# Start-up of a transformer block on one core: row tiles of x in transfers of their own, two modulation columns ahead of a transpose, one load fewer for V

## The chip, the core and the metric

The kernel runs on one core of a Trainium2 chip. The time is the device time of one execution in microseconds (us). All times inside an execution are counted from the start of its profiled span. The kernel before takes 1272.2 to 1272.4 us (medians of the jobs), and its executions on one chip lie mostly within 0.3 us of each other. The question here is about some tenths of a microsecond in the first 15 us, so the profile, which shows single events, weighs more than the timed runs. The granted clock of the tensor engine (PE) was 0.997 to 1.000.

## The reference

The reference is one block with conditioning (adaLN), attention over a cached window, and a gated feed-forward part. Only its beginning matters here.

```python
mod = (silu(c) @ w_mod)          # six vectors of 1024: sa, ca, ga, sb, cb, gb
h = layernorm(x) * (1 + ca) + sa # x: 2048 x 1024, bf16
q = h @ wq                       # 1024 x 4096: 32 heads of 128
k, v = the last 512 rows of the caches, 4 kv groups
x = x + ga * (softmax(q k^T / sqrt(128)) v @ wo)
h = layernorm(x) * (1 + cb) + sb
x = x + gb * (silu(h @ w_gate) * (h @ w_up) @ w_down)
```

## The kernel before: the parts that matter

The kernel works through x in four chunks of 512 rows, each of four row tiles of 128 rows. Tiles 0 to 3 of the first chunk stand at the very start: nothing useful can run on PE until they are loaded, normalised and transposed. SyncE issues all these loads in program order on one queue.

```python
def load_x2(i):                     # two row tiles, 512 KB, one transfer
    fetch(out=x2t[i], in_=x2d[2*i*P:2*(i+1)*P, :].rearrange("(t p) d -> p t d", p=P))

for i in range(QT // 2):            # tiles 0+1, then tiles 2+3
    load_x2(i)
for half in range(DH):
    load_wm(1, half)                # w_mod columns of ca: 1 MB, rows of 1 KB
    load_wq8(2 * half)              # weights of q, 512 KB each, rows of 2 KB
    load_wq8(2 * half + 1)
load_wm(0, 0)                       # w_mod columns of sa
...
load_wm(0, 1)
# [cut: V of group 0, two loads of wq, the transposed K]
for kv in range(1, Hkv):            # V of kv groups 1 to 3, two loads each
    load_v(kv, 0, WT // 2)
    load_v(kv, WT // 2, WT)
```

The work on the four tiles is dealt out to three engines. VectorE (DVE) takes the statistics of tiles 0, 2 and 3. ScalarE (ACT) takes sum and squares of tile 1, and 1/std of all four. GpSimd (POOL) normalises tiles 0 and 1, VectorE tiles 2 and 3. `warm(n)` are matmuls whose result is thrown away.

```python
stats_0(0); act_sum(1)              # DVE: tile 0.  ACT: sum of tile 1
nc.scalar.copy(out=siluc, in_=sil_ps)
rstd_0(0)                           # ACT, needs DVE's statistics of tile 0
stats_0(2); act_squares(1)
warm(3)
xpose_0(0, norm_0(0))               # POOL normalises, PE transposes (h_ps)
rstd_0(1, 1.0 / D); rstd_0(2)
warm(5)
stats_0(3)
xpose_0(1, norm_0(1))
xpose_0(2, ln_norm(2))              # DVE normalises
rstd_0(3)
n3 = ln_norm(3)
mod_cols(1, 0, ca1, True, (0,))     # PE: column 0 of 1+ca (mod_ps), then DVE: modT
xpose_0(3, n3)
# [cut: the tiles hs and the helper h_scale]
h_scale(0, h0_ps[0][:, 0, :])       # DVE: hs = h * (1+ca), what the first q needs
nc.scalar.copy(out=h10[:, 4:8, :], in_=h0_ps[1])
mod_cols(1, 0, ca1, True, (1,))
h_scale(1, h0_ps[0][:, 1, :])
mod_cols(1, 0, ca1, True, (2, 3))
h_scale(2, ...); h_scale(3, ...)
for dt in (0, 2):                   # DVE: copies of hT, which free a buffer for matmul results (PSUM)
    nc.vector.tensor_copy(out=h10[:, dt:dt+2, :], in_=h0_ps[0][:, dt:dt+2, :])
# then q of heads 4 to 6 (12 matmuls), then of head 0 in the buffer freed above
```

A `chain` over this whole first phase keeps program order on every engine.

## Time and profile before

| | before |
|---|---|
| time, median of the first 3 runs | 1272.22 us (1272.18 to 1272.53) |
| profiled span | 1270.4 us |
| tiles 0 and 1 of x landed | 4.48 us |
| tiles 2 and 3 of x landed | 5.83 us |
| PE transposes of tile 1 begin | 9.94 us |
| first q matmul | 12.10 us |

A landing here is the moment of the last of the 16 increments of a transfer's semaphore (the counter that the engines wait on), as the trace records them; the first increment came at 3.79 us for tiles 0 and 1 and at 5.12 us for tiles 2 and 3.

The page of the kernel before, busy time of each engine:

```profile
PE 1262.5 (99%) x7589; PEld 641.2 (50%) x7589; DVE 609.4 (48%) x1332; ACT 335.0 (26%) x440; POOL 4.2 (0%) x15
```

PE is busy for 99% of the span, so the start can only be worth the time by which PE's stream begins earlier. What sets that moment is read in the chain of waits that ended last, first 13 us, kernel before (columns: start, duration, what):

```profile
0.73 3.74 DMA x<-in_A_x_dram
4.50 1.30 DVE st L846 x2
...
6.07 0.30 ACT mv L966
...
6.72 1.25 ACT junk L982 x2
...
8.69 1.20 POOL xn L990
...
9.94 1.07 PE h_ps L961 x16
11.01 0.18 PE mod_ps L786 x8
11.19 0.47 PE h_ps L961 x8
11.66 0.58 PE mod_ps L786 x24
12.23 0.89 PE q_ps L1043 x4
```

Tile 0's statistics (`st`) wait for the joint transfer; ScalarE's chain over tile 1 (`mv`, `junk`) follows; GpSimd's rows of tile 1 (`xn`) come next; then PE has work without a pause: transposes (`h_ps`), modulation columns (`mod_ps`) and q (`q_ps`). (PE's starts in this view are modelled ends of the piece before, so the first q matmul shows as 12.23 here; its own start is 12.10.) The timeline of the kernel before shows what stood beside that chain (the bracket gives the idle time before an instruction and what ended it):

```profile
5.56 0.14 ACT L996 COPY siluc<-sil_ps 128x8 bf16<-128x8 bf16 x1
...
5.95 1.23 DVE L846 BATCH_NORM_STATS2 st<-x 128x6 f32<-128x512 bf16 x2
6.07 0.29 ACT L966 ACTIVATE mv<-mv,eps_t 128x1 f32<-128x1 f32 x1 [0.36 <-DVE mv L848]
...
8.97 1.64 DVE L865 TENSOR_SCALAR xn<-x,mv 128x1024 bf16<-128x1024 bf16 x2 [0.16 <-ACT mv L967]
...
12.10 3.73 PE L1043 MATMUL q_ps<-hs,wq 128*128 128x512 bf16 x16
...
14.79 0.33 PEld L1043 LDWEIGHTS <-wq 128*128 128x128 bf16 x3 [0.43 <-DVE hT L1032]
```

ScalarE waited for the statistics of tile 0: its copy of siluc ended at about 5.70, 1/std of tile 0 began at 6.07. VectorE began with tile 2 at 5.95 us, 0.12 us after tiles 2 and 3 had landed (5.83). And PE's thirteenth q matmul had to wait for the copies of hT: 12 matmuls of 0.216 us from 12.10 would end at 14.69, it began at 14.79.

### The profile page before, as it was taken

Reading aid. Unit: us, or ns where it says so; the run is one execution under the profiler, and the core shown is the slowest. Engines: PE = TensorE matmul, PEld = TensorE weight load, DVE = VectorE, ACT = ScalarE, POOL = GpSimd, SP = SyncE. Lnnn points to the kernel's source line nnn. Section 1 sums busy time; section 2 is a strip of 40 time slices with the busy share of each in tenths; the row PEclk is TensorE's granted clock in tenths of the full one; section 3 lists DMA queues with packets and bytes.
Section 4 is the critical chain, followed back from the end, with each engine's and each line's share of the span. In section 5 each row is a group of like instructions: output and inputs, shape, how many; then the busy total and the mean of one; then the engine's idle time right before and its main releaser. Section 6 shows DMA issues by size and latency. Waiting matters only on the chain.

```text
span 1270.4 us, 18154 instructions
## 1 busy us (share of the span) xinstructions
PE 1262.5 (99%) x7589; PEld 641.2 (50%) x7589; DVE 609.4 (48%) x1332; ACT 335.0 (26%) x440; POOL 4.2 (0%) x15
## 2 busy tenths in 40 slices
PE   8999999999999999999999999999999999999998
PEld 4555555555555555555554444444444444444444
DVE  5666658785678664677564631321122112221122
ACT  3543334343333433334341111011100111011100
POOL 1000000000000000000000000000000000000000
PEclk9999999999999999999999999999999999999999
DMA  9897667768456655454575478336633565425702
GB/s 293 204 246 188 163 141 175 166 161 222 120 137 175 150 137 154 113 154 113 121 203 146 132 229 248 95 95 209 213 115 106 169 211 183 158 91 168 246 14 72
DMA packets 306763, 204.45 MB, mean 161 GB/s; under 512 B 145521, under 2 KB 303217, under 8 KB 306674
## 3 DMA queue, kind: packets, MB, share of 16 engines
q1 hardware_dynamic: 301762, 199.03, 57.7%
q10 hardware_dynamic: 4912, 4.20, 1.0%
q8 instruction: 61, 1.00, 0.3%
q14 instruction: 28, 0.23, 0.1%
HBM read 165.94 MB, written 4.21 MB: 134 GB/s over the span
## 4 chain that ended last, share of the span: by engine, by line
PE 99%; DMA 0%; ACT 0%; DVE 0%; POOL 0%; issue 0%; POOLq 0%
PE gu_ps L1358 30%; PE a_ps L1276 17%; PE q_ps L1201 16%; PE d_ps L1378 15%; PE o_ps L1244 9%; PE s_ps L1212 9%; PE q_ps L1043 1%; DMA x<-in_A_x_dram 0%; PE one_ps L1061 0%; PE mod_ps L786 0%; PE h_ps L961 0%; PE one_ps L1054 0%; DVE st L846 0%; ACT junk L982 0%; POOL xn L990 0%; ACT mv L966 0%
## 5 line engine op out<-in xcount | busy, mean ns | idle before, releaser
L1214 ACT ACTIVATE pT<-s_ps 128x1024 bf16<-128x1024 f32 x256 | 249.3, 1020 | 347.5 <-PE s_ps L1212 347.5
L1276 PE MATMUL a_ps<-wo,oT 128*128 128x512 bf16 x1024 | 241.9, 379 | 0.0
L1201 PE MATMUL q_ps<-hT,wq 128*128 128x512 bf16 x960 | 227.1, 379 | 0.0
L1364 DVE TENSOR_TENSOR guT<-gu_ps,sg 128x512 bf16<-128x512 f32 x112 | 77.4, 691 | 286.9 <-ACT sg L1363 286.9
L1358 PE MATMUL gu_ps<-hT,wg 128*128 128x512 bf16 x896 | 211.7, 379 | 0.0
L1363 ACT ACTIVATE sg<-gu_ps 128x512 bf16<-128x512 f32 x112 | 66.9, 597 | 488.7 <-PE gu_ps L1358 483.0
L1378 PE MATMUL d_ps<-wd,guT 128*128 128x512 bf16 (+2 forms) x952 | 194.2, 366 | 0.0
L1358 PE MATMUL gu_ps<-hT,wu 128*128 128x512 bf16 x672 | 163.3, 379 | 0.0
L1276 PEld LDWEIGHTS <-oT 128*128 128x128 bf16 x1024 | 100.2, 98 | 120.6
L947 DVE CAST qT<-q_ps 128x512 bf16<-128x512 f32 x121 | 83.6, 691 | 154.9 <-PE q_ps L1201 154.7
L1201 PEld LDWEIGHTS <-wq 128*128 128x128 bf16 x960 | 93.9, 98 | 113.3
L1378 PEld LDWEIGHTS <-guT 128*128 128x128 bf16 x952 | 90.9, 98 | 103.0
L1244 PEld LDWEIGHTS <-pT 128*128 128x128 bf16 x2048 | 126.6, 98 | 30.2
L1358 PEld LDWEIGHTS <-wg 128*128 128x128 bf16 x896 | 87.6, 98 | 105.5
L1244 PE MATMUL o_ps<-v_sb,pT 128*128 128x129 bf16 x2048 | 137.0, 220 | 0.0
L1212 PE MATMUL s_ps<-qT,kT 128*128 128x512 bf16 x512 | 131.6, 379 | 0.0
L1358 PEld LDWEIGHTS <-wu 128*128 128x128 bf16 x672 | 65.8, 98 | 79.3
L1231 DVE TENSOR_TENSOR oq<-o_ps,rl 128x256 bf16<-128x256 f32 (+2 forms) x256 | 100.6, 419 | 3.9
L1382 DVE TENSOR_TENSOR f<-d_ps,gb_bc 128x512 f32<-128x512 f32 (+2 forms) x34 | 22.4, 660 | 139.8 <-PE d_ps L1378 139.8
L1212 PEld LDWEIGHTS <-kT 128*128 128x128 bf16 x512 | 44.9, 98 | 30.9 <-issue 0.5
L1284 DVE TENSOR_TENSOR acc<-a_ps,acc 128x512 f32<-128x512 f32 x64 | 44.0, 687 | 32.6 <-PE a_ps L1276 32.6
L1358 PE MATMUL gu_ps<-hT,v_sb 128*128 128x512 bf16 x224 | 57.5, 379 | 0.0
(101 smaller groups left out, 427.3 us busy)
## 6 DMA issues: line engine op xcount, KB each, us to landing
wq<-in_A_wq_dram SPq DMA_DIRECT2D x64, 512.0 KB
wo<-in_A_wo_dram SPq DMA_DIRECT2D x64, 512.0 KB
wg<-in_B_w_gate_dram SPq DMA_DIRECT2D x56, 512.0 KB
wd<-in_B_w_down_dram SPq DMA_DIRECT2D x56, 512.0 KB
wu<-in_B_w_up_dram SPq DMA_DIRECT2D x42, 512.0 KB
v_sb<-in_B_w_up_dram SPq DMA_DIRECT2D x14, 512.0 KB
x<-in_A_x_dram SPq DMA_DIRECT2D x8, 512.0 KB
wm<-in_w_mod_dram SPq DMA_DIRECT2D x4, 1024.0 KB
```

The lines of the kernel that those rows point to most:

```text
L947: nc.vector.tensor_copy(out=t, in_=q_ps)
L1201: nc.tensor.matmul(q_ps, lhsT=w, rhs=hT[("h1", cc)][:, dt, :], start=(dt == 0), stop=(dt == DT - 1))
L1212: nc.tensor.matmul(s_ps[:, i, :], lhsT=kT[:, kv, j * P:(j + 1) * P], rhs=qT[g], start=True, stop=True)
L1214: nc.scalar.activation(out=p[:, 2 * jj:2 * jj + 2, :], in_=s_ps, func=ACT.Exp, scale=scale)
L1231: nc.vector.tensor_tensor(out=dst, in0=ps[:, s0:s0 + cnt, 0:Dh], in1=sc, op=ALU.mult)
L1244: nc.tensor.matmul(o_slot["ps"][:, s_, :], lhsT=pT[g][:, j, t * P:(t + 1) * P], rhs=v_sb[:, kv, j, 0:VN], start=(j == 0), stop=(j == WT - 1))
L1276: nc.tensor.matmul(a_ps, lhsT=oT[(cc, 2 * q + i)][:, hh % 4, t * P:(t + 1) * P], rhs=wo_tiles[(cc, q, dh, i)][:, hh % 4, :], start=(hh == ...
L1284: nc.vector.tensor_tensor(out=acc[(cc, t)][:, dsl], in0=a_ps, in1=acc[(cc, t)][:, dsl], op=ALU.add)
L1358: nc.tensor.matmul(ps[:, n, :], lhsT=gu_w[(cc, fg, nm, dt // 4)][:, dt % 4, fi * P:(fi + 1) * P], rhs=hT[("h2", cc)][:, dt, :], start=(dt ...
L1363: nc.scalar.activation(out=g, in_=ps[:, 0, :], func=ACT.Silu)
L1364: nc.vector.tensor_tensor(out=guT[(cc, fg)][:, fi, :], in0=ps[:, 1, :], in1=g, op=ALU.mult)
L1378: nc.tensor.matmul(d_ps, lhsT=guT[(cc, f // 4)][:, f % 4, t * P:(t + 1) * P], rhs=wd_tiles[(cc, dh, f // 4)][:, f % 4, c0:c0 + w], start=( ...
```

## The change

The intent: tile 0 is there earlier when it does not share a transfer with tile 1, so that ScalarE's wait goes; two columns of 1+ca are ready before the last transposes, so that VectorE can scale without alternating with PE; and V of kv group 1 takes one load in place of two. The whole diff:

```diff
-    for i in range(QT // 2):
-        load_x2(i)
+    for tt in range(2):
+        fetch(out=xt[tt], in_=x2d[tt * P:(tt + 1) * P, :])
+    load_x2(1)
@@
-    for kv in range(1, Hkv):
+    load_v(1)
+    for kv in range(2, Hkv):
         load_v(kv, 0, WT // 2)
         load_v(kv, WT // 2, WT)
@@
     mod_cols(1, 0, ca1, True, (0,))
+    mod_cols(1, 0, ca1, True, (1,))
     xpose_0(3, n3)
@@
-    mod_cols(1, 0, ca1, True, (1,))
     h_scale(1, h0_ps[0][:, 1, :])
```

The order of instructions on every engine is otherwise the same, through the whole kernel.

## The prediction

> **What bounds the kernel.** One core, span 1270.4 us, and the tensor engine (PE) is busy 99% of it (busy summary). PE's waits (list of waits) are 3.2 us: 1.6 us before the first matmul and 1.6 us for normalised rows in the first 10 us; behind VectorE's copies of hT it loses 0.11 more (14.684 to 14.790). From 9.94 us on PE runs nearly without gap, so the change is worth what it brings PE's stream forward: tenths of a microsecond.
>
> **The chain before** (chain of waits, first 12 us): x tiles 0 and 1 land in one 512 KB transfer at 4.48; VectorE statistics of tile 0, 4.50 to 6.04; ScalarE rstd 0, 6.07 to 6.59, mean and squares of tile 1 to 7.97, rstd 1 to 8.53; GpSimd normalises tile 1, 8.69 to 9.89; PE transposes from 9.94. ScalarE had waited 0.36 us (5.71 to 6.07) for statistics of tile 0: only that can be gained.
>
> **Row tiles in own transfers.** The landing records show the two x transfers 1.35 us apart (4.48, 5.83), so half a transfer is 0.67 us: tile 0 should land at about 3.8, tile 1 still at about 4.5, tiles 2 and 3 at about 5.85. The Trainium skill, "DMA: Bandwidth & Descriptors" (why a DMA increments its semaphore by 16), says that only the full count tells of landing, so the joint transfer did hold tile 0 back. Statistics of tile 0 then end at 5.4, but ScalarE is bound by tile 1 (sum until 5.7): its chain gains 0.35 us, not 0.67. GpSimd's rows of tile 1 end at about 9.54. VectorE's statistics of tiles 2 and 3 gain under 0.1: tile 2 landed at 5.83 for a start at 5.95. Normalising tile 2 on VectorE took 1.19 us against 0.53 for tile 3 because it overlapped GpSimd (the Trainium skill, "SBUF — State Buffer", calls the shared ports an exclusive lock); it ended 0.28 after GpSimd, so it moves along.
>
> **Modulation columns earlier.** Same matmuls (0.2 us), moved ahead of the transposes of tile 3. With tile 1 ready 0.35 earlier, the transposes of tile 3 come only 0.15 earlier, and the first scaled rows (hs, 0.48 us after them) bind the first q matmul: about 11.88 instead of 12.10, with a new PE stall of about 0.14 us. But VectorE no longer alternates hs and modT, so its copies of hT end about 14.39 instead of 14.73, and the 0.11 us stall at 14.79 goes. Total: q of head 0 starts about 14.47 instead of 14.79, **0.3 us earlier**. Thereafter PE bound; the weights have slack (second half of w_mod's shift columns lands at 24.5, needed at 25.7).
>
> **V of kv group 1 in one load.** One issue fewer at 28 to 32 us, first used some 30 us later: 0.
>
> The main phase keeps its order on every engine, so the gain stays.
>
> **Predicted: 1271.9 us, 80% range 1271.2 to 1272.6.** Faster by over 2%: 0.005; within 2%: 0.99; slower by over 2%: 0.005.
>
> **Right if** the profile after shows VectorE's first statistics at about 3.85, ScalarE's rstd 0 at about 5.72, PE's transposes of tile 1 at 9.6, first q matmul at about 11.9, no stall behind the hT copies, all later work 0.3 us earlier. **Wrong if** the split transfers land no earlier (fixed latency rules), tile 1 or tiles 2 and 3 land later by over 0.2 us, a weight tile lands too late for PE; the spread of three runs (0.35 us) can hide it.

## The result and the profile after

The changed kernel took 1272.71 us (median of 6 runs, 1272.34 to 1274.64), the kernel before 1272.41 us in the 6 runs beside it. The ratio of the two is 1.0003 with a 95% interval of 0.9991 to 1.0016. (A ratio is the mean time of one kernel's fast runs over that of the other's of the same rounds, so not quite the ratio of the medians.) The median lies 0.1 us above the range that I had given, and the small difference has the other sign: I expected 0.3 us less. By the interval of one job this could be noise. It repeated: two further jobs gave medians of 1272.73 against 1272.38 and 1272.76 against 1272.25.

| | before | after | forecast for after |
|---|---|---|---|
| tile 0 landed | 4.48 (with tile 1) | 3.50 | 3.8 |
| tile 1 landed | 4.48 | 4.15 | 4.5 |
| tiles 2 and 3 landed (first part, last part) | 5.12, 5.83 | 5.39, **7.68** | 5.85 |
| ScalarE's 1/std of tile 0 | 6.07 | 5.27 | 5.72 |
| PE transposes of tile 1 | 9.94 | 9.14 | 9.6 |
| VectorE's statistics of tile 2 | 5.95 | **7.70** | about 5.9 |
| first q matmul | 12.10 | 12.91 | 11.88 |
| q of head 0 (thirteenth matmul) | 14.79 | 15.50 | 14.47 |
| profiled span | 1270.4 | 1271.1 | |

The chain of waits that ended last, first 13 us, kernel after:

```profile
0.74 0.40 SPq L664
...
1.19 0.42 SPq L664
...
1.66 6.01 DMA x<-in_A_x_dram
7.70 1.30 DVE st L848 x2
...
9.23 1.16 DVE st L848 x2
...
10.54 0.51 DVE xn L867
...
11.09 0.62 PE h_ps L963 x8
11.71 0.38 PE mod_ps L788 x16
12.09 0.47 PE h_ps L963 x8
12.56 0.38 PE mod_ps L788 x16
12.94 0.35 PE q_ps L1045
```

ScalarE and GpSimd are gone from it. The chain now starts with the third transfer, 6.01 us from its issue to its last part, and goes on with VectorE's statistics of tiles 2 and 3 (`st` twice) and its rows of tile 2 (`xn`). The timeline of the kernel after shows that the part that I had aimed at did work:

```profile
3.53 1.28 DVE L848 BATCH_NORM_STATS2 st<-x 128x6 f32<-128x512 bf16 x2 [1.98 <-DMA x<-in_A_x_dram]
...
5.23 0.14 ACT L998 COPY siluc<-sil_ps 128x8 bf16<-128x8 bf16 x1
5.27 0.29 ACT L968 ACTIVATE mv<-mv,eps_t 128x1 f32<-128x1 f32 x1
...
7.70 1.29 DVE L848 BATCH_NORM_STATS2 st<-x 128x6 f32<-128x512 bf16 x2 [2.64 <-DMA x<-in_A_x_dram]
...
9.14 0.62 PE L963 MATMUL h_ps<-ident,xn 128*128 128x128 bf16 x8 [0.23 <-POOL xn L992]
...
11.09 0.62 PE L963 MATMUL h_ps<-ident,xn 128*128 128x128 bf16 x8 [1.33 <-DVE xn L867]
...
12.91 2.97 PE L1045 MATMUL q_ps<-hs,wq 128*128 128x512 bf16 x12
```

ScalarE's wait is gone (no bracket at 5.27), and PE has tile 1 0.80 us earlier. The starts follow the landings by 0.02 to 0.03 us (3.50 and 3.53, 7.68 and 7.70), so the full count of 16 is indeed what the engines wait for. But VectorE then waits 2.64 us for tile 2, and PE waits 1.33 us for the rows of tile 2 (11.09). Before, tiles 2 and 3 landed 0.12 us ahead of need, so nearly all of their delay reached VectorE, and enough of it reached PE (the sum is below) that what the other chain had won went unused.

From there on both traces run in parallel. I compared every weight load of PE in the two traces: from the second half of the first phase (26 us) to the last one of the block the offset stays between +0.69 and +0.70 us. So nothing later gives or takes anything, and V of kv group 1, whose load falls at 28 to 34 us, cost or gained nothing that can be seen. The end of the kernel, behind the start of the last matmul, varies from profile to profile (4.83 to 5.19 us), and with it the span.

How fast the transfers ran is read from the windows view. The columns that matter are the last two: the busy share of the transfer engines and GB/s. The first part of the line is the window. First the kernel before, then the kernel after:

```profile
1.50:3.50 2.00, 1.91 (x5) 0.69 (x5) 0.04 (x2) 1.44 (x4) 0.26 (x1) 1.00 0.80 229
3.50:6.50 3.00, 3.00 (x10) 0.82 (x8) 1.96 (x4) 1.60 (x5) 0.52 (x5) 1.00 1.02 370
6.50:9.50 3.00, 1.61 (x14) 0.85 (x13) 2.77 (x7) 2.72 (x10) 2.16 (x3) 1.00 1.08 357
```

```profile
1.50:3.50 2.00, 1.91 (x5) 0.69 (x5) 0.05 (x2) 1.45 (x4) 0.24 (x1) 1.00 0.68 252
3.50:6.50 3.00, 2.63 (x10) 0.72 (x8) 1.49 (x3) 2.27 (x7) 1.08 (x6) 1.00 0.81 227
6.50:9.50 3.00, 2.06 (x20) 1.22 (x21) 1.76 (x4) 1.40 (x5) 2.02 (x3) 1.00 1.06 373
```

Between 3.5 and 6.5 us the transfer engines moved 370 GB/s before and 227 GB/s after, and they were partly idle although loads were waiting behind. I call this the slow stretch. It does not hit the 16 parts of a transfer alike: the first part of tiles 2 and 3 landed at 5.39, the last at 7.68. The packet records of this stretch show two things: most packets kept their usual 84 ns for 2 KB, with gaps of some 0.5 us and more between them, and some took 300 to 700 ns. (The records name neither transfer nor engine. That the gaps lie between the packets of tile 1 and those of tiles 2 and 3 is concluded from their times, 3.4 to 4.0 us.)

### The profile page after: what moved, and what is told of

Its sections match the earlier page's. It is cut to its first block, busy times and chain, and to the rows that moved or that the text cites. A ratio compares the mean times of both kernels' runs of the same rounds, so it can differ in the third digit from the quotient of the medians.

```text
span 1271.1 us, 18012 instructions
## 1 busy us (share of the span) xinstructions
PE 1254.6 (99%) x7447; PEld 641.2 (50%) x7589; DVE 609.0 (48%) x1332; ACT 335.2 (26%) x440; POOL 4.2 (0%) x15
## 4 chain that ended last, share of the span: by engine, by line
PE 98%; issue 1%; DMA 0%; DVE 0%; SPq 0%
PE gu_ps L1360 30%; PE a_ps L1278 17%; PE q_ps L1203 16%; PE d_ps L1380 15%; PE o_ps L1246 9%; PE s_ps L1214 9%; PE q_ps L1045 1%; DMA x<-in_A_x_dram 0%; DVE st L848 0%; PE one_ps L1063 0%; PE mod_ps L788 0%; PE one_ps L1056 0%; PE h_ps L963 0%; SPq L664 0%; DVE xn L867 0%
```

## Experiments

Theories at the start: (A) the late landing is chance and differs between executions; (B) the split itself causes it. Later: (S) whatever comes third, behind two short transfers, is starved; (P) it is the paired shape behind single tiles; (O) it is the third transfer of the queue, whatever precedes; (K) it is the cut to short transfers of 256 KB; (W) it is w_mod's many short rows queued behind. All kernels gave correct results. The five jobs ran on five chips; each table compares runs of one job, so of one chip.

### 1. Repeats and the parts of the change alone

`before_again` and `after_again` are the two kernels unchanged. `x_only` and `mod_only` are the kernel before with one part of the change:

```diff
 x_only:
-    for i in range(QT // 2):
-        load_x2(i)
+    for tt in range(2):
+        fetch(out=xt[tt], in_=x2d[tt * P:(tt + 1) * P, :])
+    load_x2(1)
 mod_only:
     mod_cols(1, 0, ca1, True, (0,))
+    mod_cols(1, 0, ca1, True, (1,))
     xpose_0(3, n3)
     ...
-    mod_cols(1, 0, ca1, True, (1,))
     h_scale(1, h0_ps[0][:, 1, :])
```

> The kernel before, unchanged, for a second profile. Theory A (chance: how late tiles 2 and 3 of x land differs from execution to execution, whatever the kernel): their landing differs from the first profile's 5.83 us by more than 0.2 us, or the early transfers show a slow stretch at another place. Theory B (the split itself delays tiles 2 and 3): here they land at 5.8 us again, the first q matmul starts at 12.1 us, and the span is 1270.4 us within 0.2.

> The changed kernel, unchanged, for a second profile and five timed rounds. Theory A: tiles 2 and 3 land below 6.5 us this time, the first q matmul starts at about 11.9 us, and the profiled span is about 1270.1 us; the timed runs lie on average within 0.3 us of before. Theory B: tiles 2 and 3 land after 7 us again, the first q matmul starts after 12.5 us, and the timed runs are 0.3 to 0.7 us slower than before.

> Only the split of the first x transfer. Theory A: tile 0 lands at about 3.6 us and tiles 2 and 3 at 5.8 to 6.0 us in an undisturbed execution, first q matmul at about 11.8 us, gain about 0.3 us; in a disturbed one as late as in the first profile after. Theory B: tiles 2 and 3 land after 7 us, and it is as slow as the changed kernel.

> Only the second modulation column ahead of the transposes of row tile 3. Both theories: the first q matmul starts about 0.13 us later (12.23 us), as the first scaled rows come 0.2 us later; the stall behind the copies of hT goes; from head 0 on no difference (within 0.1 us of before). Tiles 2 and 3 of x land at 5.8 us under B; anywhere from 5.8 to 8 us under A.

| run | tiles 2, 3: first, last part | first q matmul | head 0 | time, median (before beside it) |
|---|---|---|---|---|
| before_again | 5.32, 5.98 | 12.24 | 14.94 | 1272.36, 1 run (1272.38) |
| after_again | 5.15, 7.42 | 12.65 | 15.24 | 1272.73, 5 runs (1272.38) |
| x_only | 5.23, 7.68 | 12.95 | 15.63 | 1273.21, 5 runs (1272.38) |
| mod_only | 5.31, 5.97 | 12.38 | 14.97 | 1272.43, 5 runs (1272.38) |

Theory A falls: every kernel with the split lands tiles 2 and 3 1.4 to 1.9 us later than those without it, and the others agree within 0.15 us. The whole loss comes with the split (`x_only`).

`mod_only` did to the tenth what the prediction had said of the columns. They push the first scaled rows back, so the first q matmul comes 0.14 us later than in `before_again`, which had the same landing. In return the stall behind the copies of hT is gone. From head 0 on the two are 0.03 us apart: the moved columns are worth nothing here. In the split kernels they are worth something: `x_only` and the first profile of the changed kernel both had tiles 2 and 3 at 7.68, and head 0 came at 15.63 without and at 15.50 with them, as PE computes the second column while it waits for the rows of tile 3. The lines of the timeline of `mod_only`:

```profile
11.84 0.88 DVE L1022 TENSOR_SCALAR hs<-h_ps,modT 128x512 bf16<-128x512 bf16 x2
...
12.38 3.40 PE L1043 MATMUL q_ps<-hs,wq 128*128 128x512 bf16 x15
...
13.61 1.28 DVE L1032 COPY hT<-h_ps 128x1024 bf16<-128x1024 bf16 x2
```

The two scalings run back to back (`x2` at 11.84, where before they stood apart at 11.49 and 12.08), and the copies begin 1.77 us after the first scaling (13.61 less 11.84), before 1.96 us (13.45 less 11.49).

### 2. What is starved, and by what

```diff
 x4:            all four tiles in own transfers
-    for tt in range(2):
+    for tt in range(QT):
         fetch(out=xt[tt], in_=x2d[tt * P:(tt + 1) * P, :])
-    load_x2(1)
 pair_then_own: load_x2(0), then tiles 2 and 3 in own transfers
 x1_on_act:     tile 1 issued by ScalarE's queue
-        fetch(out=xt[1], ...)
+        nc.scalar.dma_start(out=xt[1], in_=x2d[P:2 * P, :])
 wm_third:      load_wm(1, 0) moved ahead of load_x2(1)
```

(The rest of each is the changed kernel. The last three edits are given in short.)

> The changed kernel with all four row tiles of x in own transfers. Theory S (short transfers at the start leave the transfer engines dry: what comes third starts late, whatever its shape): tile 2 lands late too, at 5 us or later although only 256 KB, tile 3 at 7 us or later, and the bytes moved between 3.5 and 6 us stay near 250 GB/s. Theory P (it is the paired shape coming after single tiles): no slow stretch, tile 2 at 4.8, tile 3 at 5.5 us, first q matmul at about 11.7 us, 0.3 us faster than before.

> Tiles 0 and 1 in one transfer as before, tiles 2 and 3 in own ones, the rest as changed. Theory S: the first 512 KB feed the engines until 4.4 us, so nothing runs dry: tile 3 lands by 6.0 us, the first q matmul starts near 12.3 us as with the modulation columns alone, time within 0.2 us of before. Theory P (paired after single): no paired transfer follows a single one, so no slow stretch either; if it is single tiles as such that upset what follows, w_mod's first half, which follows them, lands after 9.5 us.

> As changed, but tile 1 is issued by ScalarE's queue, so that SyncE issues tiles 2 and 3 0.45 us earlier. Theory S, if the time of issue is what makes the third transfer late: tiles 2 and 3 land by 6.2 us, tiles 0 and 1 by 4.2 us, first q matmul at about 11.7 us, about 0.3 us faster than before. If the slow stretch has another cause: tiles 2 and 3 after 7 us again.

> As changed, but w_mod's first half goes before tiles 2 and 3 of x. For telling apart, not for speed: tiles 2 and 3 land after 7.5 us in any case, the first q matmul after 12.7 us. Theory S: the slow stretch between 3.25 and 6.25 us is there again, now in w_mod, which lands its last part after 8 us. Theory P: w_mod runs at full rate from 3.5 us on (near 380 GB/s) and lands at about 7.3 us, tiles 2 and 3 slow after it.

| run | landings, first and last part | first q matmul | time, median (before beside it) |
|---|---|---|---|
| x4 | tile 2 4.63, 5.95; tile 3 5.36, 6.62 | 11.57 | 1272.28, 5 runs (1272.24) |
| pair_then_own | tile 2 4.45, 5.13; tile 3 5.17, 7.04 | 12.23 | 1272.30, 5 runs (1272.24) |
| x1_on_act | tiles 2, 3 5.24, 6.07; tile 1 5.42, 5.96 | 13.22 | 1273.18, 5 runs (1272.24) |
| wm_third | w_mod 6.92, 10.54; tiles 2, 3 8.81, 11.89 | 17.89 | 1279.65, 1 run (1272.24) |

Theory P falls with `x4` and `wm_third`. In `wm_third` w_mod stands third and is the one spread out over 3.6 us (254 GB/s between 3.5 and 6.5 us). In `x4` the slow stretch is there as well (243 GB/s between 3.5 and 5.0 us), but it is shorter, and tile 2 can start the chain before tile 3 has come. In `pair_then_own` it comes a microsecond later (237 GB/s between 4.5 and 6.5 us) and hits tile 3, which VectorE needs only at 7.35, so that it costs nothing there. Theory S falls with it: by S the 512 KB ahead should have had tile 3 landed by 6.0, and it came at 7.04. In `x1_on_act` tiles 2 and 3 were in time (359 GB/s between 3.5 and 6.5 us), but tile 1 shared the engines with them and came at 5.96 in place of 4.15, and ScalarE's chain begins with tile 1: 1 us lost, by another road.

### 3. Place in the queue or size; the other queue

`tiny1` and `tiny2` are the kernel before with one and with two loads of 4 KB ahead of x. `x4_again` is `x4`. `x23_on_act` is the changed kernel with tiles 2 and 3 issued by ScalarE, behind its small load of c:

```diff
 tiny1 (tiny2: two of them):
+    tiny0 = const.tile([P, 16], BF16, name="tiny0")
+    fetch(out=tiny0, in_=x2d[0:P, 0:16])
     for i in range(QT // 2):
         load_x2(i)
 x23_on_act:
-    load_x2(1)
+    nc.scalar.dma_start(out=x2t[1],
+        in_=x2d[2 * P:4 * P, :].rearrange("(t p) d -> p t d", p=P))
```

> The kernel before with one 4 KB load ahead of x on SyncE's queue, so that the transfer of tiles 2 and 3 is the third of the queue, as in the changed kernel, but still follows a 512 KB one. Theory O (it is the third transfer of the queue that is slow, whatever stands before it): the last part of tiles 2 and 3 lands more than 1.2 us after the first. Theory K (it is the change to short 256 KB transfers that does it): tiles 2 and 3 land within 0.8 us of each other, about 0.45 us later than before (one more issue), at 6.3 us.

> Two 4 KB loads ahead of x, so that tiles 0 and 1 are the third transfer, tiles 2 and 3 the fourth. Theory O: tiles 0 and 1 land over more than 1.2 us, after 5.5 us. Theory K: they land within 0.8 us of each other, about 0.9 us later than before (5.4 us), tiles 2 and 3 1.35 us after them.

> Four own transfers once more, for a second profile: the first had its first q matmul at 11.57 us, 0.6 us ahead of before, yet its five times averaged 0.15 us above before. If tile 2 and 3 land by 6.7 us in every execution, the q matmul starts by 11.8 us again, and the profiled run is faster than before; if executions differ, they land later this time, up to 7.5 us, and that is why the timed runs gain nothing.

> As changed, but tiles 2 and 3 are issued by ScalarE's queue, so that SyncE's third transfer is w_mod's first half. Theory O: tiles 2 and 3 land by 6.2 us without a slow stretch, while w_mod lands over more than 1.2 us; tile 1 lands at 4.8 us (it shares the engines); first q matmul at about 12 us, time within 0.2 us of before. Theory K: tiles 2 and 3 land after 7 us all the same.

| run | landings, first and last part | first q matmul | time, median (before beside it) |
|---|---|---|---|
| tiny1 | tiles 0, 1 4.50, 5.18; tiles 2, 3 5.82, 6.54 | 12.81 | 1273.26, 1 run (1272.22) |
| tiny2 | tiles 0, 1 4.65, 5.48; tiles 2, 3 6.00, 6.78; w_mod 9.07, 11.27 | 13.09 | 1274.01, 1 run (1272.22) |
| x4_again | tile 2 4.53, 5.55; tile 3 5.38, 6.27; w_mod 8.30, 10.70 | 12.12 | 1272.00, 5 runs (1272.22) |
| x23_on_act | tiles 2, 3 5.14, 5.77 | 11.67 | 1271.69, 5 runs (1272.22) |

Theory O falls with `tiny1`: tiles 2 and 3 are the third transfer of the queue and land within 0.72 us of each other (375 GB/s between 3.5 and 6.5 us). `tiny2` has a slow stretch again, but late, from 5.5 to 7.5 us (271 GB/s), in w_mod, behind both transfers of x; no theory of mine had that. Four own transfers (`x4_again`) had tile 3 in time again, but now the delay was passed on to w_mod, whose last part landed at 10.70, and PE waited 0.51 us for it ahead of the columns. So the gain of `x4` is not to be had in every execution (in the medians it was 0.04 us slower than before in one job and 0.22 us faster in the other).

`x23_on_act` is the experiment that the prediction rests on. It has the split and the moved columns, and tiles 2 and 3 land at 5.77, the time that I had assumed (5.85). The chain of waits that ended last, first 13 us, `x23_on_act`:

```profile
1.19 3.23 DMA x<-in_A_x_dram
...
4.43 1.15 ACT junk L978 x2
...
6.19 1.25 ACT junk L984 x2
...
8.15 1.21 POOL xn L992
...
9.40 1.07 PE h_ps L963 x16
10.47 0.38 PE mod_ps L788 x16
10.85 0.47 PE h_ps L963 x8
11.32 0.38 PE mod_ps L788 x16
11.70 1.43 PE q_ps L1045 x6
```

It is the chain of the kernel before again, ScalarE over tile 1 and GpSimd, only 0.54 us earlier at GpSimd's rows (8.15 against 8.69) and at PE's transposes (9.40 against 9.94). The first q matmul comes at 11.67 (forecast 11.88, before 12.10) and head 0 at 14.26 (forecast 14.47, before 14.79). The windows view of `x23_on_act`:

```profile
3.50:6.50 3.00, 3.00 (x10) 0.83 (x8) 2.20 (x5) 2.00 (x7) 0.80 (x6) 1.00 1.01 353
```

353 GB/s in place of 227, with the same two short transfers ahead on SyncE's queue. It also speaks against K and O as they were put: K had tiles 2 and 3 after 7 us here, and O had w_mod, now third on SyncE's queue, landing over more than 1.2 us (it was 0.84). That it is the second queue that helps, and not that these tiles were issued 0.26 us earlier (1.40 against 1.66 us), was not tested by itself. The time of issue alone does not bring the slow stretch, though: `tiny1` issued its tiles 2 and 3 at 1.67 us and had none, with 512 KB ahead of them.

### 4. What stands behind, and the better version again

`after_third` and `x23_act_again` are repeats. `x23_act_old_cols` is `x23_on_act` with the second column back where it was. `wq_first` is the changed kernel with the loads of wq ahead of w_mod:

```diff
 wq_first:
-    for half in range(DH):
-        load_wm(1, half)
-        load_wq8(2 * half)
-        load_wq8(2 * half + 1)
+    for i in range(2):
+        load_wq8(i)
+    for half in range(DH):
+        load_wm(1, half)
+    for i in range(2, 4):
+        load_wq8(i)
```

> As changed, but two loads of wq (2 KB rows, 256 of them each) stand behind tiles 2 and 3 of x in place of w_mod's first half (1 KB rows, 1024 of them), which follows. Theory W (the many short rows of w_mod, queued behind tiles 2 and 3, hold their rows up): tiles 2 and 3 land by 6.2 us. If not W: after 7 us again, over more than 1.5 us. The time is worse than before in both cases, as w_mod lands after 11 us.

> The changed kernel for a third profile and five more times, beside the version with tiles 2 and 3 on ScalarE's queue: tiles 2 and 3 land between 7 and 8 us, the timed runs 0.2 to 0.7 us slower than before.

> The version with tiles 2 and 3 on ScalarE's queue once more. If its gain was no luck of one job: tiles 2 and 3 land by 6 us, the first q matmul starts by 11.8 us, the timed runs are 0.3 to 0.6 us faster than before and about 1 us faster than the changed kernel.

> The same with the modulation column back behind the transposes of tile 3. By the argument of the prediction the first q matmul starts 0.1 us earlier (11.6 us), but the stall behind the copies of hT is back (about 0.1 us), so that from head 0 on it is within 0.1 us of the version with the columns moved. If the moved columns were worth their intent, it is 0.2 us slower.

| run | tiles 2, 3: first, last part | first q matmul | head 0 | time, median (before beside it) |
|---|---|---|---|---|
| wq_first | 5.39, 8.59 | 16.09 | | 1277.28, 1 run (1272.25) |
| after_third | 5.51, 7.32 | 12.56 | 15.14 | 1272.76, 5 runs (1272.25) |
| x23_act_again | 5.14, 6.57 | 11.81 | 14.40 | 1271.94, 5 runs (1272.25) |
| x23_act_old_cols | 5.09, 6.40 | 11.67 | 14.35 | 1271.85, 5 runs (1272.25) |

Theory W falls: without w_mod's short rows behind them tiles 2 and 3 come even later (195 GB/s between 3.5 and 6.5 us). The loss of the changed kernel repeats. The gain of the other queue repeats in the medians (0.31 and 0.40 us), but hardly in the means (0.06 and 0.18 us), as the spread is wider: single executions of the two versions with ScalarE's queue reached 1273.24 and 1273.02 us. Some of the 16 parts were late here, too, against the 6 us that I had expected: in `x23_act_again` two of them landed at 6.44 and 6.57, where the others had landed by 5.50, and the transfer ruled again. The columns can't be judged from head 0 of the two as it stands, since the landings differ by 0.17 us. From the last landing to head 0 it is 7.83 us with the columns moved (14.40 less 6.57; 7.82 in all three profiles of the changed kernel) and 7.95 us without (14.35 less 6.40; the same in `x_only`, 15.63 less 7.68). So where the late tiles rule, the columns are worth 0.12 to 0.13 us; my expectation of under 0.1 us, and that of an effect of the opposite sign on the first q matmul alone, told only the case of tiles in time (`mod_only`).

### 5. Bytes or rows, one or two

```diff
 col_halves:    two transfers of 256 KB again, but each of both tiles and half the columns
+    for hf in range(2):
+        fetch(out=x2t[0][:, :, hf*512:(hf+1)*512],
+              in_=x2d[0:2*P, hf*512:(hf+1)*512].rearrange("(t p) d -> p t d", p=P))
 x1_after_x23:  tile 0, then load_x2(1), then tile 1
```

> As changed, but the first 512 KB are halved by columns, not by row tiles: two transfers of 256 KB again, each with 256 rows of 1 KB instead of 128 rows of 2 KB. If it is the bytes of the transfers at the start that matter, tiles 2 and 3 land after 7 us again. If it is the number of rows in a transfer (128 against 256), they land by 6.3 us. Tiles 0 and 1 are both ready only with the second half, at 4.5 us.

> As changed, but tile 1 goes behind tiles 2 and 3. If one short transfer ahead is enough for the slow stretch, tiles 2 and 3 land over more than 1.2 us; if it takes two in a row, they land by 5.5 us within 0.8 us, and tile 1 by 6.2 us. The time is worse than before in both cases, as ScalarE's chain begins with tile 1: about 1 us or more.

`col_halves` landed tiles 2 and 3 from 5.55 to 7.25 us (250 GB/s between 3.5 and 6.5 us): it is not the 128 rows of a transfer, since these had 256. In `x1_after_x23` tiles 2 and 3 landed from 4.46 to 5.22, without delay; tile 1, third, from 5.13 to 6.39, with 235 GB/s between 4.5 and 6.0 us. One short transfer ahead of the pair thus leaves the pair alone, and the slow stretch comes behind it. I had forecast tile 1 by 6.2 us if it takes two short transfers in a row; it missed that, so two in a row are not needed for a slow stretch. Their single times, 1272.57 and 1273.70 us against 1272.08, are as expected of late tiles.

**What is shown, and what stays open.** Shown: the two short transfers at the head of SyncE's queue bring a slow stretch of up to about 3 us, in all nine profiles of the six kernels that start SyncE's queue with two transfers of 256 KB and send tiles 2 and 3 over the same queue (the changed kernel three times, `x_only`, `x4` twice, `wm_third`, `wq_first`, `col_halves`), whatever stands third; with 1.5 us it was shortest in `x4`; with tiles 2 and 3 issued from the other queue it is gone from the rate (353, 364 and 342 GB/s between 3.5 and 6.5 us in three profiles), though single parts were still late in two of them. Two short transfers are not the only way to a slow stretch: `pair_then_own`, `x1_after_x23` and `tiny2` had one too, later and behind other sequences. Open: the mechanism. I have no view of the descriptors on their way to the engines. Place in the queue, shape, rows per transfer and what stands behind are each refuted as its cause by one profile or two; "short transfers" alone does not explain why `tiny1` has no slow stretch and `tiny2` a late one.

## Why the prediction was wrong, point by point

- **What bounds the kernel: right.** PE's stream runs without a pause behind the first phase, and the offset at 26 us (+0.7) is still there at the end.
- **Tile 0 earlier, and ScalarE's wait of 0.36 us gone: right, and undersized.** Tile 0 landed at 3.50 (forecast 3.8) and tile 1 at 4.15 (forecast 4.5): the first 512 KB came in 0.33 us faster in two transfers than in one. GpSimd's rows of tile 1 came 0.80 us earlier (7.89 against 8.69), where I had counted 0.35. The sum closes: 0.35 counted, 0.33 by the faster landing, and 0.12 because I had let 1/std of tile 0 start behind the end of ScalarE's copy (5.70 before), while the traces show it starting 0.04 us after that copy's start (5.27 after 5.23), so the wait of 0.36 us was really one of about 0.47 us.
- **"tiles 2 and 3 at about 5.85": wrong. This is the step that failed.** They landed at 7.68, 7.42 and 7.32 us in the three profiles of the changed kernel. I had split one transfer's time in proportion to its bytes and had assumed that the transfers behind would follow at the same rate, 1.35 us for 512 KB. The trace before could not show otherwise, since no short transfer stood there at the start. The path that the prediction had kept, from tile 1 over ScalarE and GpSimd to PE, therefore no longer set PE's start; the third transfer and VectorE's work on tiles 2 and 3 did. Why that transfer is late stays open. The prediction did name "tiles 2 and 3 land later by over 0.2 us" among what would make it wrong, and its range gave it little room.
- **What the delay cost: follows from the chain.** In all three profiles the first q matmul comes 5.23 or 5.24 us after the last part of tiles 2 and 3 (12.91 less 7.68, 12.65 less 7.42, 12.56 less 7.32). Before, it came 6.27 us after them, since the other chain ruled. So of a delay of 1.85 us about 1.04 us was hidden and 0.81 us was paid at the first q matmul (12.91 against 12.10). Most of what was hidden lies in VectorE's rows of tile 2: they began 1.57 us later (10.54 against 8.97), but took 0.49 us in place of 1.19, since GpSimd had finished, and so ended only 0.88 us later.
- **The columns: right for tiles that are in time.** The first q matmul later by 0.14 us (`mod_only`), the stall of 0.10 us behind the hT copies gone, nothing left from head 0 on. In the changed kernel as it ran they saved 0.13 us of the loss, since PE had to wait for tile 3 anyway; the prediction had not looked at that case.
- **The lock between VectorE and GpSimd: right.** The Trainium skill, "SBUF — State Buffer", section "Who interferes with whom", says that the pair of ports that VectorE shares with GpSimd is an exclusive lock. The trace agrees that VectorE waits: the rows of tile 2 took 1.19 us beside GpSimd and ended 0.28 us after it, 0.99 us in `x23_on_act`, ending 0.28 us after it again, and 0.49 us in the changed kernel, where GpSimd had finished. It does not show a full block up to GpSimd's recorded end, from which the whole 0.49 us should have followed and not 0.28; by its legend the profile's spans of GpSimd are rough.
- **V: right as far as seen.** No offset appears where its loads stand; it was not run by itself.
- **Once the failed step is put right, the rest holds.** With tiles 2 and 3 at 5.77 us (`x23_on_act`) the first q matmul came at 11.67 and the median at 1271.69 us against 1272.22. My sum had said 0.32 us at head 0; it was 0.53 (14.26 against 14.79). The rest is again 0.12 us of ScalarE's pipelined start and 0.07 us of tile 1's landing (4.41 against 4.48). In the medians that version was 0.53 and 0.31 us below the kernel before in two jobs, and 0.82 us below the changed kernel in the one that had both. The 95% intervals of the ratio to before (0.9983 to 1.0010, and 0.9987 to 1.0014) do not exclude that there is no difference, so the gain in time is likely, not shown. The first job's five runs (1271.52 to 1272.03) all lie below the nine of before beside them (1272.04 to 1272.28); the second's do not.

## What to carry to other kernels

When a transfer at the head of a queue is cut so that its first part comes earlier, look at when the transfers behind it land, and at how much slack they had: here the first tile gained 1 us and the next pair, which had 0.12 us of slack, lost 1.5 to 1.9. The bytes divided by the usual rate do not size the first microseconds of a queue; one profile of the cut does. If what stands behind is needed soon, try giving it to another engine's queue, but check what it then competes with: for tiles 2 and 3 this won 0.3 to 0.5 us in the medians, for tile 1 it lost one microsecond.

## What the Trainium skill lacked or had wrong

- "DMA: Bandwidth & Descriptors", section "Issuing engines are not separate DMA queues", says that starting transfers from several engines only saves the sequencer's time to initiate them. Here tiles 2 and 3 were issued 0.26 us earlier on ScalarE's queue (1.40 against 1.66 us) and landed 0.8 to 1.9 us earlier (5.77, 6.57 and 6.40 against 7.68, 7.42 and 7.32 us).
- No page tells of a slow stretch behind short transfers at the start of a queue: 227 GB/s against 370 GB/s between 3.5 and 6.5 us, with the 16 parts of one transfer landing over 1.8 to 2.3 us in place of 0.7 us. The section "Queues, rings and completion order" of the same page would be the place.
- The fit of time against size in the same page, section "Anatomy of one DMA", is for transfers issued by GpSimd. For the first transfer on SyncE's queue these runs show, from issue to last landing, 1.63 us for 4 KB (`tiny1`), 2.76 us for 256 KB (after) and 3.75 us for 512 KB (before).
- "SBUF — State Buffer", section "Who interferes with whom", agreed with the trace in that the rows wait for GpSimd (1.19 us beside GpSimd against 0.49 us without). The page has the loser blocked fully; here the rows ended 0.28 us after GpSimd's recorded end, and not their whole 0.49 us after it.
